# Exponentials per head straight from PSUM with bias and sum, a scaled magnitude of the weight words, and lo parts of two weight matrices on VectorE in the first tile

## The chip, the core and the metric

The kernel runs on one core of one Trainium2 chip. A core has a matrix engine (TensorE, PE, which loads a stationary operand, then streams a moving one and writes to PSUM), a vector engine (VectorE, DVE), an engine for pointwise functions (ScalarE, ACT), a general engine (GpSimd, POOL) and a queue engine (SyncE, SP) that here issues all the DMAs. Each engine takes its own instructions in the order of the program and waits by semaphores for the others. The metric is device time in microseconds, the median of several runs. The profile is of one execution.

## The reference

Attention over pooled keys and values, and a feed-forward layer on its output. Cut to what is computed:

```python
# q, k, v: (8 batches, 8 heads, 576, 64) float32; pool = 8, Sp = 72
k_p = k.reshape(B, H, Sp, pool, D).mean(axis=3)
v_p = v.reshape(B, H, Sp, pool, D).mean(axis=3)
scores = scale * np.matmul(q, k_p.transpose(0, 1, 3, 2))
scores = scores - np.max(scores, axis=-1, keepdims=True)
attn = np.exp(scores)
attn = attn / (np.sum(attn, axis=-1, keepdims=True) + 1e-09)
out = np.matmul(attn, v_p)                     # then (B*S, H*D) = (4608, 512)
...
a = x @ w_a                                    # 512 -> 1536
b = x @ w_b
return (a * b @ w_out).astype(np.float32)      # 1536 -> 512
```

The weights reach the kernel as 64-bit floats, seen as pairs of 32-bit words, and the kernel makes 32-bit floats of them.

## The kernel before

**Two parts for every operand.** Each matrix product is made of three matmuls: every operand is split into a hi part, a copy to the matmul's type (ACT), and a lo part, what is left of it, a subtraction (`low_part`, L170, on DVE or POOL as its caller says). The products are hi by hi, hi by lo and lo by hi, summed in PSUM.

**The feed-forward part.** The 4608 rows are nine tiles of 512. For each tile, twelve steps x run over the 1536 middle columns in blocks of 128 (`ffn_in`, L539, and `ffn_out`, L560). A step has 12 matmuls into `psa`, 12 into `psb` and, for the step before, 12 into the four `acc` banks; ACT copies `psa` to `h` (L555), DVE multiplies `h` by `psb` (L528), ACT and DVE make the parts `hh` and `hl` (L531, L171). `split_weight` makes the parts of the weight blocks, `jh` on ACT (L236) and `jl` on POOL (L238, recorded as L171), anew for each tile.

**The weights' conversion.** Only in the first tile, `convert_weights` turns the words of 36 blocks (twelve each of `a`, `b`, `o`) into floats: ACT takes the magnitude of the high word (L212) and scales the low word (L213), DVE limits and scales the magnitude (L214), masks and shifts it (L215), puts the sign back (L219) and adds the low word (L224). The load of the next block's words (L222) follows L219, as the words have one buffer per matrix.

**The attention part.** The rows of a batch are five chunks of 128 rows, one of them with 64; there are 40 chunks, and `chunk(i)` carries one from its queries to the transposed probabilities. Chunks 0 to 4 come before the first tile's feed-forward, the others are spread between the matmuls of the tile before the one that needs them. The scores of a chunk are made from `kdiag`, the pooled keys of two heads side by side in hi and lo parts. Chunks below SUMMED = 9 make them in two halves of four heads, 6 matmuls of 144 columns each, and take maximum and difference from PSUM (L374, L375 in `less_max`). Chunks from 9 on use per pair of heads one matmul of 288 columns (the query's hi part by both parts of the keys side by side) and one of 144, add the two halves of columns on DVE (L410), and then take maximum and difference for all heads from SBUF. Then one exponential for all eight heads (L424, ACT), the sum (L426), 1e-9 and the reciprocal (L427, L428, DVE), the product (L430, POOL mostly), the parts of the probabilities `pr` and `rem` (L439, L441 on ACT, lo parts on POOL), and the transposes on PE (L475, copied out by ACT at L476). Scores, transposes and values of later chunks share two PSUM buffers of the tag `att`.

**What sets the order.** The order is written out by hand. `Chains` holds generators; `chains.step()` is called six times in each step x, every six matmuls, and resumes the chains that are due. `yield n` puts the rest of a chain n steps later, `yield PE` waits for a turn to put matmuls into the stream (one chain a step in the feed-forward part). What a chain issues between two yields stands together in the program, and each engine meets it in that order.

Of the kernel before, what the change touches and what calls it, by code (L numbers as in the profile page):

```python
# [9 lines left out]
F32 = mybir.dt.float32  # L10
F32R = mybir.dt.float32r
I32 = mybir.dt.int32
U32 = mybir.dt.uint32
AF = mybir.ActivationFunctionType
ALU = mybir.AluOpType
# [5 lines left out]
P = 128  # L21
# [7 lines left out]
TINY = 2.0**-15  # L29
# [25 lines left out]

SUMMED = 9
# [57 lines left out]
def attn_moe_kernel(ctx: ExitStack, tc: tile.TileContext, q, k, v, vr, wa, wb, wo, out):  # L114
# [55 lines left out]
    def low_part(eng, lo, src, hi):  # L170
        eng.tensor_tensor(out=lo, in0=src, in1=hi.bitcast(F32), op=ALU.subtract)  # L171
# [23 lines left out]
    def convert_weights(name, j, first):  # L195
# [4 lines left out]

# [5 lines left out]
        for f in range(NF):  # L206
# [5 lines left out]
            nc.scalar.activation(mag, hi.bitcast(F32), AF.Abs)  # L212
            nc.scalar.activation(low, lo.bitcast(U32), AF.Copy, scale=2.0**-29)  # L213
            nc.vector.tensor_scalar(out=w, in0=mag, scalar1=TINY, scalar2=2.0**-16, op0=ALU.max, op1=ALU.mult)  # L214
            nc.vector.tensor_scalar(  # L215
                out=wi, in0=wi, scalar1=0x0FFFFFFF, scalar2=3, op0=ALU.bitwise_and, op1=ALU.logical_shift_left
# [14 lines left out]
    def split_weight(name, x):  # L231
# [6 lines left out]
        low_part(nc.gpsimd, lo, raw[name][:, f, :], hi)  # L238
# [107 lines left out]
    def chunk(i):  # L346
# [25 lines left out]
        def less_max(hs, src):  # L372
            nh = hs.stop - hs.start
            nc.vector.tensor_reduce(out=m[:n, hs], in_=src, axis=AX.X, op=ALU.max)  # L374
            nc.vector.tensor_tensor(  # L375
                out=s[:n, hs], in0=src, in1=m[:n, hs].unsqueeze(2).broadcast_to([n, nh, SP]), op=ALU.subtract
            )

        if i < SUMMED:
            for g0 in range(0, NK, 2):  # L380
                yield from wait(("keys", b, g0))
                yield PE
                if first:
                    pt = ps.tile([P, 512], F32, tag="acc", name=f"psc_{i}_{g0}", bufs=4)
                else:
                    pt = ps.tile([P, 512], F32, tag="att", name=f"psc_{i}_{g0}", bufs=2)
                for j in range(2):
                    g = g0 + j
                    for x, (qq, w) in enumerate(((qh, 0), (qh, 1), (ql, 0))):
                        nc.tensor.matmul(  # L390
                            pt[:n, j * hk:(j + 1) * hk],
                            qq[:, g, :n],
                            kd[:, g, w].rearrange("p e s -> p (e s)"),
                            start=(x == 0),
                            stop=(x == 2),
                        )
                less_max(slice(2 * g0, 2 * g0 + 4), pt[:n, :2 * hk].rearrange("p (h s) -> p h s", h=4))
        else:
            for g in range(NK):
                yield from wait(("keys", b, g - g % 2))  # L400
                if g % 2 == 0:
                    yield PE
                pt = ps.tile([P, 512], F32, tag="att", name=f"psc_{i}_{g}", bufs=2)
                nc.tensor.matmul(  # L404
                    pt[:n, :2 * hk], qh[:, g, :n], kd[:, g].rearrange("p w e s -> p (w e s)"), start=True, stop=False
                )
                nc.tensor.matmul(
                    pt[:n, :hk], ql[:, g, :n], kd[:, g, 0].rearrange("p e s -> p (e s)"), start=False, stop=True
                )
                nc.vector.tensor_reduce(  # L410
                    out=s[:n, 2 * g:2 * g + 2, :].rearrange("p h s -> p (h s)"),
                    in_=pt[:n, :2 * hk].rearrange("p (w c) -> p c w", w=2),
                    axis=AX.X,
                    op=ALU.add,
                )
                if g % 2 and g < NK - 1:
                    yield 1
            yield 1
            less_max(slice(0, H), s[:n])
# [264 lines left out]
```

## Time and profile before

| | |
|---|---|
| median of 3 runs | 1110.5 us (1110.24 to 1191.36) |
| the profiled execution | 1109.42 us, its span 1107.6 us |
| mean granted clock of PE | 0.972 |
| busy, share of the span | PE 94%, weight loads 78%, DVE 54%, ACT 47%, POOL 51% |
| the chain that ended last | PE 82%, DVE 13%, ACT 2% of the span |
| read from memory, written | 49.28 MB, 9.44 MB |

A line of the profile has the program's line, the engine, the operation, the tile written and the tiles read, and the shapes. Busy time is the sum of the durations; matmuls overlap in the records, so two of them follow each other faster than one lasts, and PE's pace is read from start to start. Shares over the whole span mix stages with different limits, so that the stage has to be named with each number.

### The profile page before, as it was taken

Reading aid. Unit: us, or ns where it says so; the run is one execution under the profiler, and the core shown is the slowest. Engines: PE = TensorE matmul, PEld = TensorE weight load, DVE = VectorE, ACT = ScalarE, POOL = GpSimd, SP = SyncE. Lnnn points to the kernel's source line nnn. Section 1 sums busy time; section 2 is a strip of 40 time slices with the busy share of each in tenths; the row PEclk is TensorE's granted clock in tenths of the full one; section 3 lists DMA queues with packets and bytes.
Section 4 is the critical chain, followed back from the end, with each engine's and each line's share of the span. In section 5 each row is a group of like instructions: output and inputs, shape, how many; then the busy total and the mean of one; then the engine's idle time right before and its main releaser. Section 6 shows DMA issues by size and latency. Waiting matters only on the chain.

```text
span 1107.6 us, 13659 instructions
## 1 busy us (share of the span) xinstructions
PE 1036.8 (94%) x4964; PEld 861.5 (78%) x4964; DVE 601.3 (54%) x953; ACT 523.2 (47%) x1051; POOL 565.4 (51%) x465
## 2 busy tenths in 40 slices
PE   4378887899999999999999999999999999999998
PEld 4256765688887888888888888888888888888887
DVE  8889899963348333753367335653458343332111
ACT  3654555544445445544455445444445444443332
POOL 6234353455555555555555455554556455554442
PEclk9778888999999999999999999999999999999999
DMA  6444343220023000400021002200211020001001
GB/s 221 124 142 124 121 129 120 74 89 1 1 70 111 1 1 22 148 3 1 1 94 59 1 1 91 81 1 1 69 55 48 1 67 1 1 1 38 1 1 38
DMA packets 29875, 59.59 MB, mean 54 GB/s; under 512 B 7121, under 2 KB 7121, under 8 KB 29809
## 3 DMA queue, kind: packets, MB, share of 16 engines
q1 hardware_dynamic: 29808, 58.73, 16.7%
q8 instruction: 39, 0.64, 0.2%
q14 instruction: 28, 0.22, 0.1%
HBM read 49.28 MB, written 9.44 MB: 53 GB/s over the span
## 4 chain that ended last, share of the span: by engine, by line
PE 82%; DVE 13%; ACT 2%; DMA 1%; issue 1%; POOL 0%; SPq 0%; DVEq 0%; ACTq 0%
PE acc L571 9%; PE psa L550 8%; PE psb L550 8%; PE acc L573 8%; PE acc L572 8%; PE psa L552 8%; PE psa L551 8%; PE psb L551 8%; PE psb L552 8%; PE ptr L475 2%; PE psc L404 2%; DVE wb_raw L224 1%; DVE wa_raw L224 1%; DVE wo_raw L224 1%; DVE wb_raw L219 1%
## 5 line engine op out<-in xcount | busy, mean ns | idle before, releaser
L171 POOL TENSOR_TENSOR jlb<-wb_raw,jhb 128x512 fp32r<-128x512 f32 x108 | 142.8, 1322 | 244.6 <-ACT jhb L236 244.6
L528 DVE TENSOR_TENSOR h<-psb,h 128x512 f32<-128x512 f32 x108 | 74.5, 690 | 344.1 <-PE psb L552 334.3
L171 POOL TENSOR_TENSOR jla<-wa_raw,jha 128x512 fp32r<-128x512 f32 x108 | 143.1, 1325 | 196.4 <-ACT jha L236 170.1
L555 ACT COPY h<-psa 128x512 f32<-128x512 f32 x108 | 63.3, 587 | 241.9 <-PE psa L552 234.3
L550 PE MATMUL psb<-xh,jhb 128*128 128x512 f32 x432 | 172.9, 400 | 4.6 <-DVE h L528 4.6
L571 PE MATMUL acc<-jho,hh 128*128 128x512 f32 x432 | 175.7, 407 | 0.0
L550 PE MATMUL psa<-xh,jha 128*128 128x512 f32 x432 | 172.7, 400 | 0.0
L573 PE MATMUL acc<-jho,hl 128*128 128x512 f32 x432 | 170.2, 394 | 0.6 <-DVE hl L171 0.6
L572 PE MATMUL acc<-jlo,hh 128*128 128x512 f32 x432 | 170.0, 393 | 0.0
L552 PE MATMUL psb<-xh,jlb 128*128 128x512 f32 x432 | 170.0, 393 | 0.0
L551 PE MATMUL psb<-xl,jhb 128*128 128x512 f32 x432 | 169.9, 393 | 0.0
L552 PE MATMUL psa<-xh,jla 128*128 128x512 f32 x432 | 169.6, 392 | 0.0
L551 PE MATMUL psa<-xl,jha 128*128 128x512 f32 x432 | 169.3, 392 | 0.0
L171 POOL TENSOR_TENSOR jlo<-wo_raw,jho 128x512 fp32r<-128x512 f32 x108 | 154.3, 1428 | 5.6 <-ACT jho L236 5.6
L531 ACT CAST hh<-h 128x512 fp32r<-128x512 f32 x108 | 67.1, 621 | 84.7 <-DVE h L528 84.6
L171 DVE TENSOR_TENSOR hl<-h,hh 128x512 fp32r<-128x512 f32 x108 | 93.9, 869 | 20.7 <-ACT hh L531 20.5
L550 PEld LDWEIGHTS psb<-xh,jhb 128*128 128x128 f32 x432 | 82.2, 190 | 20.9 <-issue 4.3
L573 PEld LDWEIGHTS acc<-jho,hl 128*128 128x128 f32 x432 | 81.9, 190 | 18.9 <-DVE hl L171 1.0
L552 PEld LDWEIGHTS psb<-xh,jlb 128*128 128x128 f32 x432 | 82.2, 190 | 17.6
L552 PEld LDWEIGHTS psa<-xh,jla 128*128 128x128 f32 x432 | 81.7, 189 | 17.6
L551 PEld LDWEIGHTS psb<-xl,jhb 128*128 128x128 f32 x432 | 82.2, 190 | 15.2
L551 PEld LDWEIGHTS psa<-xl,jha 128*128 128x128 f32 x432 | 82.0, 190 | 15.2 <-DVE xl L171 0.2
(92 smaller groups left out, 1714.4 us busy)
## 6 DMA issues: line engine op xcount, KB each, us to landing
out<-y SPq DMA_DIRECT2D x36, 256.0 KB, 2.2
kraw<-in_k SPq DMA_DIRECT2D x28, 288.0 KB, 3.6
vraw<-in_v SPq DMA_DIRECT2D x28, 256.0 KB, 3.0
qraw<-in_q SPq DMA_DIRECT2D x28, 256.0 KB, 3.7
words<-in_wa SPq DMA_DIRECT2D x12, 512.0 KB, 3.5
words<-in_wb SPq DMA_DIRECT2D x12, 512.0 KB, 3.6
words<-in_wo SPq DMA_DIRECT2D x12, 512.0 KB, 3.5
vraw<-in_vr SPq DMA_DIRECT2D x14, 192.0 KB, 2.5
```

Source lines behind the costliest of these rows:

```text
L171: eng.tensor_tensor(out=lo, in0=src, in1=hi.bitcast(F32), op=ALU.subtract)
L224: nc.vector.tensor_tensor(out=wi, in0=wi, in1=low, op=ALU.add)
L404: nc.tensor.matmul(pt[:n, :2 * hk], qh[:, g, :n], kd[:, g].rearrange("p w e s -> p (w e s)"), start=True, stop=False)
L528: nc.vector.tensor_tensor(out=h, in0=pt, in1=h, op=ALU.mult)
L531: nc.scalar.copy(hh, h)
L550: nc.tensor.matmul(pt, wh[:, c], xh[:, kk], start=(kk == 0), stop=False)
L551: nc.tensor.matmul(pt, wh[:, c], xl[:, kk], start=False, stop=False)
L552: nc.tensor.matmul(pt, wl[:, c], xh[:, kk], start=False, stop=(kk == NK - 1))
L555: nc.scalar.copy(h, pt)
L571: nc.tensor.matmul(acc[c], hh[:, cs], wh, start=(f == 0), stop=False)
L572: nc.tensor.matmul(acc[c], hh[:, cs], wl, start=False, stop=False)
L573: nc.tensor.matmul(acc[c], hl[:, cs], wh, start=False, stop=(f == NF - 1))
```

## The change

Four things change.

1. In `convert_weights` the magnitude is scaled by 2^-112 in ACT's instruction, and the DVE instruction that limited it from below and scaled it (L214) is gone; the mask and the shift read ACT's result directly.
2. In `split_weight` the lo parts of `a` and `b` are made on VectorE for the twelve blocks of the first tile. Those of `o`, and all of the later tiles, stay on GpSimd.
3. All chunks make their scores as chunks 0 to 8 did, in two halves of four heads; SUMMED and the other way are gone.
4. In each half DVE takes the maximum and multiplies it by -SCALE; ACT then makes one exponential per head, from PSUM, with that as its bias and with the sum over the head's 72 columns as a second output. The difference, the one exponential over all heads and DVE's sum are gone, and with them two places where the chain gave way for a step.

```diff
-TINY = 2.0**-15
+SHRINK = 2.0**-112
...
-SUMMED = 9
...
-            nc.scalar.activation(mag, hi.bitcast(F32), AF.Abs)
+            nc.scalar.activation(mag, hi.bitcast(F32), AF.Abs, scale=SHRINK)
             nc.scalar.activation(low, lo.bitcast(U32), AF.Copy, scale=2.0**-29)
-            nc.vector.tensor_scalar(out=w, in0=mag, scalar1=TINY, scalar2=2.0**-16, op0=ALU.max, op1=ALU.mult)
             nc.vector.tensor_scalar(
-                out=wi, in0=wi, scalar1=0x0FFFFFFF, scalar2=3, op0=ALU.bitwise_and, op1=ALU.logical_shift_left
+                out=wi, in0=mag.bitcast(I32), scalar1=0x0FFFFFFF, scalar2=3, op0=ALU.bitwise_and, op1=ALU.logical_shift_left
             )
...
-        low_part(nc.gpsimd, lo, raw[name][:, f, :], hi)
+        low_part(nc.vector if x < NF and name != "o" else nc.gpsimd, lo, raw[name][:, f, :], hi)
...
-        def less_max(hs, src):
-            nh = hs.stop - hs.start
-            nc.vector.tensor_reduce(out=m[:n, hs], in_=src, axis=AX.X, op=ALU.max)
-            nc.vector.tensor_tensor(
-                out=s[:n, hs], in0=src, in1=m[:n, hs].unsqueeze(2).broadcast_to([n, nh, SP]), op=ALU.subtract
-            )
-
-        if i < SUMMED:
-            for g0 in range(0, NK, 2):
...
-                less_max(slice(2 * g0, 2 * g0 + 4), pt[:n, :2 * hk].rearrange("p (h s) -> p h s", h=4))
-        else:
-            for g in range(NK):
...
-            yield 1
-            less_max(slice(0, H), s[:n])
+        for g0 in range(0, NK, 2):
+            yield from wait(("keys", b, g0))
+            yield PE
+            if first:
+                pt = ps.tile([P, 512], F32, tag="acc", name=f"psc_{i}_{g0}", bufs=4)
+            else:
+                pt = ps.tile([P, 512], F32, tag="att", name=f"psc_{i}_{g0}", bufs=2)
+            for j in range(2):
+                g = g0 + j
+                for x, (qq, w) in enumerate(((qh, 0), (qh, 1), (ql, 0))):
+                    nc.tensor.matmul(
+                        pt[:n, j * hk:(j + 1) * hk],
+                        qq[:, g, :n],
+                        kd[:, g, w].rearrange("p e s -> p (e s)"),
+                        start=(x == 0),
+                        stop=(x == 2),
+                    )
+            hs = slice(2 * g0, 2 * g0 + 4)
+            scores = pt[:n, :2 * hk].rearrange("p (h s) -> p h s", h=4)
+            nc.vector.tensor_reduce(out=m[:n, hs], in_=scores, axis=AX.X, op=ALU.max)
+            nc.vector.tensor_scalar_mul(m[:n, hs], m[:n, hs], -SCALE)
+            for j in range(4):
+                h = 2 * g0 + j
+                nc.scalar.activation(
+                    s[:n, h], scores[:, j], AF.Exp, bias=m[:n, h:h + 1], scale=SCALE, accum_out=z[:n, h:h + 1]
+                )
         mark("scores", i)
 
 
         yield 1
-        nc.scalar.activation(s[:n], s[:n], AF.Exp, scale=SCALE)
-        yield 1
-        nc.vector.tensor_reduce(out=z[:n], in_=s[:n], axis=AX.X, op=ALU.add)
         nc.vector.tensor_scalar_add(z[:n], z[:n], 1e-9)
         nc.vector.reciprocal(z[:n], z[:n])
         yield 1
```

More of the change, by code (lines that the diff above doesn't have):

```diff
@@ L370, in chunk @@
         hk = 2 * SP
-        def less_max(hs, src):
-            nh = hs.stop - hs.start
-            nc.vector.tensor_reduce(out=m[:n, hs], in_=src, axis=AX.X, op=ALU.max)
-            nc.vector.tensor_tensor(
-                out=s[:n, hs], in0=src, in1=m[:n, hs].unsqueeze(2).broadcast_to([n, nh, SP]), op=ALU.subtract
-            )
-        if i < SUMMED:
-            for g0 in range(0, NK, 2):
[L381 to L384, printed above, removed]
-                else:
[L386 to L396, printed above, removed]
-                less_max(slice(2 * g0, 2 * g0 + 4), pt[:n, :2 * hk].rearrange("p (h s) -> p h s", h=4))
-        else:
-            for g in range(NK):
[L400 to L405, printed above, removed]
-                )
[L407 to L416, printed above, removed]
-                    yield 1
-            yield 1
-            less_max(slice(0, H), s[:n])
@@ L420, in chunk @@
         mark("scores", i)
         yield 1
-        nc.scalar.activation(s[:n], s[:n], AF.Exp, scale=SCALE)
-        yield 1
-        nc.vector.tensor_reduce(out=z[:n], in_=s[:n], axis=AX.X, op=ALU.add)
         nc.vector.tensor_scalar_add(z[:n], z[:n], 1e-9)
```

## The prediction

> **What bounds the kernel now.** I read the page's slices first, then the table by stage, then who waited in the slow stage, and only then single groups.
>
> ```profile
> span 1107.6 us, 13659 instructions
> PE   4378887899999999999999999999999999999998
> DVE  8889899963348333753367335653458343332111
> PEclk9778888999999999999999999999999999999999
> ```
>
> The reader is to see two stages. In the first eight slices VectorE (DVE) is at 8 or 9 tenths, and TensorE (PE) is neither full nor at full clock. From then on PE is at 9 to the end and DVE at 3 to 7. The table by stage gives it in microseconds (columns: busy time of PE, weight loads, DVE, ACT, POOL, each with its count; then the granted clock and the DMA share):
>
> ```profile
> core 0: us, PE busy (x) PEld busy (x) DVE busy (x) ACT busy (x) POOL busy (x), PEclk, DMA share, GB/s
> 36.00:60.00 24.00, 8.99 (x50) 8.31 (x49) 19.55 (x33) 12.04 (x24) 4.32 (x4) 0.64 0.57 178
> 60.00:216.00 156.00, 123.57 (x550) 98.64 (x548) 142.12 (x208) 85.59 (x170) 67.08 (x49) 0.86 0.38 119
> 216.00:1107.60 891.60, 887.66 (x4295) 739.70 (x4294) 409.04 (x659) 408.90 (x820) 472.77 (x382) 1.00 0.11 34
> ```
>
> From 36 to 216 us, the first tile with its weight conversion, DVE is busy 161.7 of 180 us (19.55 and 142.12). What DVE no longer does there comes off the end nearly one for one. After 216 us PE is busy 887.66 of 891.60 us at full clock: what DVE, ACT or POOL save there is worth nothing, and each microsecond added to PE is paid in full. The change must be read against both stages.
>
> **The change part by part: VectorE in the first tile.** Each row below comes from a line's own view (count: shortest/median/longest ns), and the row under it is that line's busy DVE time in the window 36 to 216 us.
>
> ```profile
> L214 DVE TENSOR_SCALAR wa_raw<-wmag_a x12: 367/420/1516, 34.9 to 194.6; 128x512 f32<-128x512 f32 x12
> 36.00:216.00 180.00, 19.53 (x35) 0.83 0.41 127
> ...
> L215 DVE TENSOR_SCALAR wa_raw<-wa_raw x12: 426/427/2510, 35.3 to 195.0; 128x512 int32<-128x512 int32 x12
> 36.00:216.00 180.00, 20.83 (x35) 0.83 0.41 127
> ...
> L219 DVE SCALAR_TENSOR_TENSOR wa_raw<-words,wa_raw x12: 641/694/1810, 36.3 to 195.5; 128x512 int32<-128x512 int32 x12
> 36.00:216.00 180.00, 31.87 (x36) 0.83 0.41 127
> ...
> L224 DVE CUSTOM_DVE_ANT_0 wa_raw<-wa_raw,wlow_a x12: 691/693/3084, 37.8 to 197.4; 128x1024 uint16<-128x1024 uint16 x12
> 36.00:216.00 180.00, 39.60 (x36) 0.83 0.41 127
> ```
>
> (a) The words' magnitude. L214 goes from DVE: 19.53 us in the window. ACT's L212 takes the scale as one more immediate of an instruction that is there already, so I add nothing to it; at a tenth of its length more, ACT, far from full here, would cover it. The load of the next words (L222, on SP's queue) is issued behind L219 and so a little earlier; the pace of the conversion is held by `begun`, not by the load.
>
> (b) The lo parts of `a` and `b` for x below 12 go from POOL to DVE, 24 instructions. The nearest DVE row is `hl`, the same operation, shape and types:
>
> ```profile
> L171 POOL TENSOR_TENSOR jla<-wa_raw,jha x13: 1264/1296/1717, 41.1 to 214.5; 128x512 fp32r<-128x512 f32 x13
> L171 POOL TENSOR_TENSOR jlo<-wo_raw,jho x11: 1269/1705/1743, 68.2 to 211.3; 128x512 fp32r<-128x512 f32 x11
> L171 DVE TENSOR_TENSOR hl<-h,hh x11: 676/684/1786, 76.5 to 214.3; 128x512 fp32r<-128x512 f32 x11
> L171 DVE TENSOR_TENSOR hl<-h,hh 128x512 fp32r<-128x512 f32 x11 | 9.7, 879 | 0.0
> ```
>
> Between its median and its mean, 0.78 us, 24 cost 18.7 us (bounds 16.4 at 0.684 and 21.1 at 0.879). Alone, (a) and (b) nearly cancel.
>
> (c) What comes with (b): DVE instructions here have two lengths. L224 takes 0.693 us or up to 3.08, L215 0.427 or up to 2.51. Over their medians, L215 has 20.83 - 35 x 0.427 = 5.9 us, L219 31.87 - 36 x 0.694 = 6.9 and L224 39.60 - 36 x 0.693 = 14.7: 27.5 us of waiting inside DVE instructions, in lumps of about the 1.3 us that a POOL subtraction takes. I read it as DVE and POOL keeping each other out. POOL has 53 instructions in these 180 us (4 and 49); 24 go, so I take 24/53 of 27.5 = 12.4 us off. Bounds: 0, if the other POOL work meets DVE instead, and 27.5.
>
> By the Trainium skill (SBUF — State Buffer, "Who interferes with whom") a VectorE instruction with two SBUF inputs, or in a 2-port mode, and a GpSimd instruction that reads SBUF exclude each other for a whole instruction, and whichever starts first wins. The two lengths agree with it. It also says that the moved subtractions, having two SBUF inputs, stay exposed to `jlo`, which is why I did not price them at the bare median.
>
> (d) Softmax on DVE, chunks 0 to 8:
>
> ```profile
> L426 DVE TENSOR_REDUCE z<-s x9: 736/741/754, 16.1 to 190.1; 128x8 f32<-128x576 f32 x7, 64x8 f32<-64x576 f32 x2
> L375 DVE TENSOR_TENSOR s<-psc,m x18: 450/458/459, 11.4 to 186.9; 128x288 f32<-128x288 f32 x14, 64x288 f32<-64x288 f32 x4
> L374 DVE TENSOR_REDUCE m<-psc x18: 441/448/458, 10.9 to 186.4; 128x4 f32<-128x288 f32 x14, 64x4 f32<-64x288 f32 x4
> L427 DVE TENSOR_SCALAR z<-z x9: 162/172/1032, 16.9 to 190.9; 128x8 f32<-128x8 f32 x7, 64x8 f32<-64x8 f32 x2
> 0.00:36.00 36.00, 2.64 (x4) 1.00 0.55 178
> 36.00:216.00 180.00, 1.53 (x5) 0.83 0.41 127
> ```
>
> Gone: 9 x 0.741 + 18 x 0.458 = 14.9 us. New: 18 small multiplications by -SCALE, whose nearest row is L427 (its busy time stands under it: 4.17 us for nine, 0.46 each): 8.3 us. Net -6.6 us; bounds -11.8 (all at 0.172) and +3.7 (all at 1.032). L374 stays. The skill's rule in that section speaks against the change here: the subtraction that goes reads PSUM and by the rule never meets POOL (450 to 459 ns agrees), while the multiplication that comes works from SBUF and can be held (162 to 1032 ns agrees); if every one were held, the end would be 10.3 us later than by my mean.
>
> DVE in the first 216 us: -19.5 + 18.7 - 12.4 - 6.6 = -19.8 us, taken as **-20**.
>
> **ACT.** One exponential per chunk becomes eight, of 72 elements, with a pointer bias and a sum. The trace has no such instruction; the nearest are the small copy and the exponential itself:
>
> ```profile
> L441 ACT CAST rem<-s 128x64 fp32r<-128x64 f32 x64 | 12.4, 241 | 0.0
> L424 ACT ACTIVATE s<-s 128x576 f32<-128x576 f32 x32 | 22.0, 688 | 45.0 <-DVE s L375 44.8
> ```
>
> The two give 0.87 ns an element, so at least 0.25 us each; writing out the sum at most another instruction of that size, 0.50. A gain is excluded, as one 688 ns instruction is all that goes. Between the ends I take 0.4, nearer the upper one, since bias and sum both come on top: eight take 3.2 us, 2.5 more per chunk. For the 31 later chunks that is 78 us on an engine busy 409 of 892; for the first nine 23 us. Hidden as busy time, but not as latency: ACT now waits in program order for PE's scores, DVE's maximum and the new multiplication, twice per chunk, with the weights' copies, `h` and `hh` queued behind; DVE's L427 waits for the eight in turn, with PSUM evictions behind it. If ACT had no room the first tile would get the 23 us back.
>
> The Trainium skill (ScalarE: Activation LUTs, "What ACT_TABLE_LOAD costs") gives 280 ns + 0.833 per element with a pointer bias and about 93 ns of overlap, an estimated 0.25 us at 72 elements; it has no price for the sum. By it eight cost 2.0 us and the sum of the forecast is the same.
>
> **TensorE after 216 us.** With SUMMED gone, chunks 9 to 39 form scores as the first nine did: per half six matmuls of 144 columns in place of two of 288 and two of 144. First matmul of a half and the first one behind it, new form and then old form, both at full clock in the feed-forward stream:
>
> ```profile
> 183.33 0.34 PE L390 MATMUL psc<-kdiag,qh 128*128 128x144 f32 x2
> 183.96 0.43 PE L550 MATMUL psb<-xh,jhb 128*128 128x512 f32 x1
> ...
> 217.94 0.29 PE L404 MATMUL psc<-kdiag,qh 128*128 128x288 f32 x1
> 218.39 0.44 PE L550 MATMUL psb<-xh,jhb 128*128 128x512 f32 x1
> ...
> L404 PE MATMUL psc<-kdiag,qh x124: 293/295/403, 215.6 to 969.9; 128*128 128x288 f32 x100, 128*64 128x288 f32 x24
> ```
>
> 0.63 against 0.45 us: +0.18 per half. The 100 full matmuls of L404 are 50 halves: **+9.0 us**; the 24 on 64 rows I put at nothing (at the same 0.18 they would add 2.2). No cover: PE is the bound.
>
> **The latency behind it.** The new code drops two steps between scores and transposes. In an old chunk:
>
> ```profile
> 410.76 0.29 PE L404 MATMUL psc<-kdiag,qh 128*128 128x288 f32 x1
> 417.69 0.20 DVE L428 RECIPROCAL z<-z 128x8 f32<-128x8 f32 x1
> 421.92 0.32 POOL L171 TENSOR_TENSOR rem<-s,rem 128x64 fp32r<-128x64 f32 x1
> 424.00 0.46 PE L475 MATMUL ptr<-ident,pr 128*128 128x128 f32 x4
> 425.77 0.47 PE L475 MATMUL ptr<-ident,pr 128*128 128x128 f32 x4
> ```
>
> The reciprocal ends at +7.1, the lo parts at +11.5, the second transposes start at +15.0. Two steps of about 1.4 us fewer (36 matmuls make six steps) and 0.36 us more PE work put those at +12.6, so the reciprocal must end by 12.6 - 4.4 = +8.2. New: scores 0.6, maximum and multiplication 0.9, eight exponentials 3.2, three other ACT copies between them at some 0.6, z 0.4: about +7. It fits with 1 us to spare. The PSUM buffers (two, `att`) are held through the exponentials; where a 64-row chunk follows closely on another they may be missed. I add **+2 us** for such places (bounds 0 and 8, some 2 us at four places).
>
> **Sum.** The profiled execution took 1109.4 us (span 1107.6), 1.1 below the median of 1110.5. 1109.4 - 20 + 9 + 2 = 1100.4, so 1100.
>
> **The rivals.**
> - *More of the waiting inside DVE goes, and PE's clock with it.* For: PEclk is 0.86 there, and the lumps sit in the pairs that move. Against: 29 POOL instructions stay. With all 27.5 us gone instead of 12.4: 1085. Chance 0.17. By the skill's exclusion rule the lumps cannot go while `jlo` stays, which is why this is not higher.
> - *ACT becomes the late one in the first tile* (its waits for the maxima hold up `jha`, which DVE now waits for in order, where POOL waited before). For: 45 us of idle before L424 already. Against: ACT is busy only 85.6 of 156. If three quarters of the gain are lost: 1109.4 - 5 + 11 = 1115. Chance 0.17.
> - *Slower: PE waits for the transposes in every later chunk.* The place is ptr L475; it starts when the eight exponentials push the reciprocal past +8.2, at about 0.55 us each, and every further 0.1 us costs 0.8 us x 31 = 25 us. At 0.75 us each: 1150; the limit of slower is crossed near 0.7. Against: my upper row gives 0.50. Chance 0.08.
> - *The exchange does nothing*: gains and PE's 11 us just cancel, 1109. It lies within the forecast's own range.
>
> **How the numbers follow.** Forecast 1100, chance 0.58, own range 1092 to 1109. With the rivals at 1085 and 1115 inside, the range is 1084 to 1118; it leaves out the slower case and some of the tails, about 0.2. Two per cent, about what a measurement of this kernel can tell from no change, is 22 us: faster means below 1088, slower above 1133. Faster 0.19 (the first rival and the edge of the forecast), slower 0.09, same 0.72.
>
> **What would show it.** L214 gone; 24 lo parts on DVE near 0.7 to 0.8 us; means of L219 and L224 lower by a third to a half; first-tile stage ending near 196 us instead of 216; PE from there to the end 11 us longer, with halves of 0.63 us; eight exponentials per chunk of 0.25 to 0.5 us; no ptr wait on PE after the first tile. I am wrong if the stage ends after 210 us (ACT), or if ptr L475 waits in most chunks, or if the 144-column halves cost PE no more than before.

## The result, and the profile after

The changed kernel takes 1118.9 us (median of 4 runs, 1116.7 to 1121.0) against 1111.0 us for the kernel before in the same comparison: a ratio of 1.0073, 95% interval 1.0048 to 1.0099. It is within 2%, on the slow side, and 0.9 us above the predicted range. One of the four runs before took 1191.4 us in a slow state of the chip; its median counts this run, the ratio does not, and the same holds for one run of e9 below (1465.5 us, at a granted clock of 0.67). The profiled execution of the changed kernel took 1116.7 us, with a span of 1115.0 us.

The first view of the changed kernel's page is the busy table and the slices, as quoted of before:

```profile
span 1115.0 us, 14406 instructions
...
PE   4387888999998999999999999999999999999998
...
DVE  7688888632455225632456335643356333332111
...
PEclk9989889999999999999999999999999999999999
```

The reader is to see that VectorE's run of 8s and 9s is shorter and lower than before, and that PE's slices behind it look the same but for one 8, the slice from 334 to 362 us. At this grain no more of the loss is visible. I cut both traces at the same three events instead: the first feed-forward matmul of step 0, the first one of step 12 (the end of the first tile), and the last matmul. Columns as in the prediction's table by stage, first of before, then of after:

```profile
59.70:223.90 164.20, 131.63 (x588) 105.38 (x588) 149.88 (x220) 89.12 (x177) 70.29 (x51) 0.86 0.37 113
223.90:1103.40 879.50, 879.50 (x4258) 733.21 (x4257) 400.63 (x647) 405.17 (x814) 469.56 (x379) 1.00 0.11 33
```

```profile
59.90:209.20 149.30, 127.72 (x591) 101.89 (x591) 123.88 (x207) 100.99 (x268) 37.16 (x29) 0.92 0.40 125
209.20:1110.70 901.50, 892.41 (x4378) 745.80 (x4377) 377.12 (x553) 457.64 (x1263) 477.44 (x380) 1.00 0.10 33
```

The first tile became 14.9 us shorter (164.2 to 149.3), the rest 22.0 us longer (879.5 to 901.5). Their sum, with 0.2 us at the start, is the 7.4 us by which the span grew. So there are two questions. In the first tile DVE's busy time fell by 26.0 us (149.88 to 123.88), yet the stage by only 14.9: the idle time of DVE, length less busy, rose from 14.3 to 25.4 us. And in the rest PE has 12.9 us more busy time (892.41 against 879.50) and 9.1 us in which it does nothing, where before it had none.

**First tile: who waits.** The list of waits from 36 us to the end of that stage (microseconds in all, times, longest), first of before, then of after:

```profile
DVE wa_raw L214 <- ACT wmag_a L212: 2.8, 3, 1.3
DVE wo_raw L214 <- ACT wmag_o L212: 2.4, 3, 1.0
DVE wb_raw L214 <- ACT wmag_b L212: 2.0, 2, 1.3
...
ACT s L424 <- DVE s L375: 11.9, 5, 4.3
```

```profile
ACT s L392 <- DVE m L389: 20.6, 11, 3.9
...
DVE z L399 <- ACT s L392: 7.8, 6, 1.5
DVE wa_raw L212 <- ACT wmag_a L210: 5.6, 3, 3.4
DVE wo_raw L212 <- ACT wmag_o L210: 5.3, 3, 2.5
DVE wb_raw L212 <- ACT wmag_b L210: 4.9, 3, 1.9
```

DVE waits 15.8 us for ACT's magnitudes where it waited 7.2, and 7.8 us for the sums, a wait it did not have. ACT in turn stands 20.6 us before exponentials, waiting for DVE's maxima. The two engines wait for each other in turn. The program puts the words' magnitudes behind exponentials on ACT, so one that waits for its maximum holds them up; e8 tests how much of the loss this is.

**The rest: halves and transposes.** The halves cost what the prediction read off chunks 0 to 8 (first matmul of a half, and the first one behind it, in the timeline of after):

```profile
257.50 0.35 PE L379 MATMUL psc<-kdiag,qh 128*128 128x144 f32 x2
...
258.13 0.44 PE L522 MATMUL psa<-xh,jha 128*128 128x512 f32 x1
```

0.63 us. The list of waits from 220 us on has this PE row, and that of before has none for the same stretch:

```profile
PE ptr L447 <- ACT p L448: 7.7, 5, 3.5
```

The timeline of after around one of these waits (start, length, instruction, and in brackets the idle time before it), by engine:

```profile
335.57 1.49 POOL L402 TENSOR_TENSOR s<-s,z 64x576 f32<-64x576 f32 x1 [4.40 <-DVE z L400]
337.02 1.29 POOL L170 TENSOR_TENSOR jla<-wa_raw,jha 128x512 fp32r<-128x512 f32 x1
338.40 1.36 POOL L170 TENSOR_TENSOR pr<-s,pr 64x512 fp32r<-64x512 f32 x1
339.71 0.33 POOL L170 TENSOR_TENSOR rem<-s,rem 64x64 fp32r<-64x64 f32 x1
339.99 1.28 POOL L170 TENSOR_TENSOR jlb<-wb_raw,jhb 128x512 fp32r<-128x512 f32 x1
341.24 1.25 POOL L170 TENSOR_TENSOR jlo<-wo_raw,jho 128x512 fp32r<-128x512 f32 x1
...
335.97 6.81 DVE L328 SCALAR_TENSOR_TENSOR vdiag<-vp,vdiag 64x256 fp32r<-64x256 f32 x2
342.70 0.68 DVE L170 TENSOR_TENSOR vrem<-vwide,vrem 32x512 fp32r<-32x512 f32 x1
343.41 0.69 DVE L500 TENSOR_TENSOR h<-psb,h 128x512 f32<-128x512 f32 x1
...
344.13 0.62 ACT L503 CAST hh<-h 128x512 fp32r<-128x512 f32 x1 [4.18 <-DVE h L500]
344.66 0.64 ACT L448 CAST p<-ptr 128x256 fp32r<-128x256 f32 x2
...
345.17 0.36 PE L447 MATMUL ptr<-ident,rem 64*96 64x64 f32 x2 [3.52 <-ACT p L448]
```

Read from the bottom: PE stands 3.52 us at the third group of transposes, which needs a buffer that ACT's copies of the first two groups (L448) must free. ACT had been idle for 4.18 us, but these copies stand behind `hh`, which waits for `h` from DVE. And DVE is in two small instructions on the values' diagonals (`vdiag`), 6.81 us for the two. Meanwhile, from 335.57 to 342.49 us, POOL works through six instructions with gaps of at most 0.1 us: the product of a 64-row chunk, its two lo parts and the weights' three. The line's own view (count, then shortest/median/longest ns, 300 to 1100 us) gives a `vdiag` a median of 1.68 us after, and below it, from the trace of before, 0.42:

```profile
L328 DVE SCALAR_TENSOR_TENSOR vdiag<-vp,vdiag x10: 915/1684/4149, 336.0 to 853.6; 64x256 fp32r<-64x256 f32 x10
```

```profile
L331 DVE SCALAR_TENSOR_TENSOR vdiag<-vp,vdiag x10: 404/422/1461, 345.4 to 846.8; 64x256 fp32r<-64x256 f32 x10
```

In the trace the diagonals are made once for each batch, at six places from 208 us on. At three of them a 64-row chunk's share of POOL falls on them, and the two instructions take 4.3 to 6.8 us; at the other three it is the weights' subtractions beside a 128-row chunk, and they take 2.4 us. That the two dropped steps moved this work there was at this point a reading of one trace. The experiments had to test it, and to divide the 22.0 us.

The wait of 3.52 us has a tail. Before it PE's feed-forward matmuls start every 0.23 us, behind it (346.05, 346.48, 346.90 us and on) every 0.43 us, and the granted clock there is half. A second such stretch comes after the wait of 1.55 us that ends at 858.72 us (windows, same columns):

```profile
345.17:348.30 3.13, 3.13 (x9) 2.38 (x10) 0.31 (x1) 0.91 (x3) 1.28 (x1) 0.50 0.00 0
860.30:863.60 3.30, 3.30 (x14) 2.67 (x13) 0.61 (x2) 1.30 (x8) 0.87 (x1) 0.51 0.00 0
```

Outside these two stretches no microsecond from 210 to 1100 us has a clock under 0.96, and in the traces of before, of e4 and of e5 none has one under 0.97. At half the clock these 6.4 us do the work of 3.2, so a part of the loss stands in PE's busy time and not in its waits. A wait of 1.54 us at 601 us has no such stretch behind it; what sets one off is not shown.

### The profile page after: what moved, and what is told of

It reads as the page before. It is cut to its first block, busy times and chain, and to the rows that moved or that the text cites. A ratio compares the mean times of both kernels' runs of the same rounds, so it can differ in the third digit from the quotient of the medians.

```text
span 1115.0 us, 14406 instructions
## 1 busy us (share of the span) xinstructions
PE 1045.9 (94%) x5088; PEld 870.9 (78%) x5088; DVE 543.8 (49%) x839; ACT 594.8 (53%) x1651; POOL 538.6 (48%) x441
## 3 DMA queue, kind: packets, MB, share of 16 engines
q1 hardware_dynamic: 29808, 58.73, 16.5%
## 4 chain that ended last, share of the span: by engine, by line
PE 78%; DVE 13%; ACT 6%; issue 2%; DMA 1%; SPq 0%; DVEq 0%; ACTq 0%
PE psb L522 8%; PE psa L522 8%; PE psa L524 8%; PE psa L523 8%; PE acc L543 8%; PE acc L544 8%; PE acc L545 8%; PE psb L524 8%; PE psb L523 7%; PE psc L379 3%; ACT s L392 3%; DVE vdiag L328 2%; PE ptr L447 2%; DVE vrem L170 1%; DVE h L500 1%
## 5 line engine op out<-in xcount | busy, mean ns | idle before, releaser
L170 POOL TENSOR_TENSOR jlb<-wb_raw,jhb 128x512 fp32r<-128x512 f32 x96 | 125.1, 1303 | 201.2 <-ACT jhb L233 201.2
L522 PE MATMUL psb<-xh,jhb 128*128 128x512 f32 x432 | 177.8, 412 | 1.3 <-DVE h L500 1.3
L543 PE MATMUL acc<-jho,hh 128*128 128x512 f32 x432 | 171.5, 397 | 0.0
L392 ACT ACTIVATE s<-psc,m 128x72 f32<-128x72 f32 (+1 forms) x320 | 97.9, 318 | 133.1 <-DVE m L389 131.7
L170 POOL TENSOR_TENSOR jla<-wa_raw,jha 128x512 fp32r<-128x512 f32 x96 | 138.4, 1442 | 44.1 <-ACT jha L233 43.7
L402 POOL TENSOR_TENSOR s<-s,z 128x576 f32<-128x576 f32 (+1 forms) x38 | 46.1, 1213 | 223.7 <-PE psb L524 141.0
L170 DVE TENSOR_TENSOR hl<-h,hh 128x512 fp32r<-128x512 f32 x108 | 125.8, 1165 | 38.2 <-ACT hh L503 38.0
L543 PEld LDWEIGHTS acc<-jho,hh 128*128 128x128 f32 x432 | 81.9, 190 | 16.2
```

Source lines behind the costliest of these rows:

```text
L392: nc.scalar.activation(s[:n, h], scores[:, j], AF.Exp, bias=m[:n, h:h + 1], scale=SCALE, accum_out=z[:n, h:h + 1])
L402: (nc.vector if first and i % 2 else nc.gpsimd).tensor_tensor(out=s[:n], in0=s[:n], in1=z[:n].unsqueeze(2).broadcast_to([n, H, SP]), op=AL ...
L522: nc.tensor.matmul(pt, wh[:, c], xh[:, kk], start=(kk == 0), stop=False)
L543: nc.tensor.matmul(acc[c], hh[:, cs], wh, start=(f == 0), stop=False)
```

## The experiments

All twelve experiments, first as a table. The first tile and the rest are the lengths between the events named above, from each profiled execution. The kernel before is at 1110.5 to 1110.6 us in each comparison. Parts 1 to 4 are those of the section on the change.

| kernel | first tile | rest | median us | ratio, 95% interval |
|---|---|---|---|---|
| before | 164.2 | 879.5 | 1110.5 | 1 |
| after | 149.3 | 901.5 | 1118.9 | 1.0073 (1.0048 to 1.0099) |
| e1 parts 1 and 2 | 145.1 | 879.5 | 1088.8 | 0.9800 (0.9785 to 0.9815) |
| e2 after, later chunks as before | 148.9 | 879.6 | 1094.3 | 0.9850 (0.9835 to 0.9864) |
| e3 after, chunks 0 to 8 as before | 144.8 | 903.0 | 1112.6 | 1.0018 (1.0008 to 1.0027) |
| e4 part 3 alone | 164.7 | 889.0 | 1120.2 | 1.0082 (1.0065 to 1.0099) |
| e5 after, two steps put back | 148.8 | 892.2 | 1108.2 | 0.9981 (0.9972 to 0.9991) |
| e6 after, later products on DVE | not cut | 900.3 | 1113.2 | 1.0039 (1.0021 to 1.0056) |
| e7 part 1 alone | 149.5 | 879.6 | 1096.6 | 0.9881 (0.9865 to 0.9898) |
| e8 e2, exponentials a step later | 145.1 | 879.6 | 1089.5 | 0.9816 (0.9801 to 0.9832) |
| e9 part 2 alone | 156.2 | 879.6 | 1101.7 | 0.9921 (0.9901 to 0.9941) |
| e10 after, corrections of e5 and e8 | 143.0 | 892.3 | 1102.3 | 0.9927 (0.9910 to 0.9944) |
| e11 e1, all three lo parts on DVE | 141.6 | 879.5 | 1085.2 | 0.9779 (0.9761 to 0.9797) |
| e12 e11, new softmax in chunks 0 to 8 | 143.0 | 879.6 | 1088.3 | 0.9799 (0.9783 to 0.9816) |

### e1: parts 1 and 2 alone

The kernel before with the first two parts; scores and softmax stay as they were.

```diff
-            nc.scalar.activation(mag, hi.bitcast(F32), AF.Abs)
+            nc.scalar.activation(mag, hi.bitcast(F32), AF.Abs, scale=SHRINK)
...
-            nc.vector.tensor_scalar(out=w, in0=mag, scalar1=TINY, scalar2=2.0**-16, op0=ALU.max, op1=ALU.mult)
...
-        low_part(nc.gpsimd, lo, raw[name][:, f, :], hi)
+        low_part(nc.vector if x < NF and name != "o" else nc.gpsimd, lo, raw[name][:, f, :], hi)
```

> The kernel before with parts 1 and 2 alone (scaled magnitude, lo parts of a and b on VectorE in the first tile), softmax as before. Theory A (in the changed kernel VectorE's work of the first tile fell by 27 us, but 12 of them came back as idle time because ScalarE, held by the new exponentials, is late): without the exponentials VectorE falls by about 22 us and its idle time stays near 18, so twelve steps end near 204 us of the span instead of 223.9, and the time is near 1091 us. Rival B (the idle time is the next limit, the loads of the words and the pace of the steps, and comes whoever relieves VectorE): twelve steps end near 210 us and the time is near 1097 us.

Measured: 1088.8 us, with the twelfth step ending at 203.9 us: theory A. The two stages of its trace, same columns:

```profile
58.80:203.90 145.10, 126.53 (x588) 101.82 (x587) 131.58 (x212) 88.86 (x177) 38.87 (x29) 0.93 0.42 128
203.90:1083.40 879.50, 879.50 (x4258) 733.25 (x4257) 399.20 (x647) 405.14 (x814) 470.07 (x379) 1.00 0.10 33
```

The rest is that of before, and the first tile is 19.1 us shorter. All of the change's gain sits in parts 1 and 2. Against this kernel, the new scores and softmax take another 7.7 us of busy time off DVE in the first tile (131.58 to 123.88), but the stage gets 4.2 us longer, because the idle time of DVE goes from 13.5 to 25.4 us.

### e2 and e3: the new softmax in one stage only

In e2 chunks 9 to 39, in e3 chunks 0 to 8 go back to the scores and softmax of before; the rest is the changed kernel.

```diff
-        for g0 in range(0, NK, 2):
-            yield from wait(("keys", b, g0))
...
+        if i < SUMMED:
+            for g0 in range(0, NK, 2):
+                yield from wait(("keys", b, g0))
...
+        else:
+            for g in range(NK):
+                yield from wait(("keys", b, g - g % 2))
```

(e3 has `i >= SUMMED` in the first condition. After the `else` both have the code of before, shortened here.)

> The changed kernel, but chunks 9 to 39 form scores and softmax as before. Theory: the first tile is as in the changed kernel (13 to 15 us gained) and the 22 us lost after it are gone, so about 1097 us. Rival: part of the later loss is a shift that the first tile hands on; then it stays above 1105 us.

> The changed kernel, but chunks 0 to 8 have the softmax as before, so the first tile is that of parts 1 and 2 alone, and chunks 9 to 39 have the new one. Theory A: first tile as in the run with parts 1 and 2 alone (near 204 us at twelve steps), then 22 us lost: about 1113 us. Rival B: first tile near 210 us, 1119 us.

Measured: 1094.3 us, 3 us less than its theory said, and 1112.6 us, as theory A said. The rest of e2 is 879.6 us, that of before, and that of e3 is 903.0, near that of after (901.5); the first tiles are 148.9 and 144.8 us. The new softmax costs in both places: some 4 us in the first tile, where it was to gain 6.6, and, with the halves, some 22 us later.

### e4: part 3 alone

All chunks form their scores in two halves, with the softmax and the steps of before.

```diff
-SUMMED = 9
+SUMMED = 40
```

> The kernel before with the scores of all chunks in halves of six matmuls, maximum and difference from PSUM as chunks 0 to 8 do, one exponential, sum on VectorE; one step fewer from scores to transposes than before, two more instructions of VectorE per chunk, no other part of the change. Theory: the halves cost 0.18 us each, 9 to 10 us in all, and no long waits of transposes come: 1120 to 1121 us, with the six-transpose groups near their 17.7 us in all. Rival (the long waits come with the dropped step and not with the exponentials on ScalarE): 1126 to 1131 us, with single waits over 1 us at the transposes of the 64-row chunks.

Measured: 1120.2 us, 9.7 more than before, and in the trace

```profile
224.90:1113.90 889.00, 888.27 (x4378) 742.74 (x4377) 373.64 (x583) 403.41 (x812) 471.82 (x380) 1.00 0.10 33
```

9.5 us more than before (889.00 against 879.50), with PE busy all but 0.7 us of it. These are the halves, and one of the two dropped steps goes with them, as the expectation says; by itself it brings no long waits. Of the 22.0 us, 12.5 are left for what the halves are not: 8.4 us more in which PE does nothing (9.1 against 0.7) and 4.1 us more in which it is busy (892.41 against 888.27), of which the two stretches at half clock are some 3.2.

### e5: the two dropped steps put back

```diff
         mark("scores", i)
-        yield 1
+        yield 1 if i < 9 else 3
         nc.vector.tensor_scalar_add(z[:n], z[:n], 1e-9)
```

> The changed kernel with the two dropped steps put back for chunks 9 to 39, ahead of the addition of 1e-9, so that product, parts and transposes are issued where they were before. The changed kernel lost 10 us at the third group of transposes of six chunks (single waits of 1.2 to 4.8 us). Theory S (the waits come from the dropped steps, which bring two chunks' work and a batch's values together): the waits go and the time falls by some 10 us, to 1108 to 1110 us. Rival P (they come from GpSimd's instructions piling up behind the product that waits for the sums, and VectorE being shut out while the pile runs off): part of it stays, as the product still waits for the eight sums, but with more time; 1112 to 1119 us.

Measured: 1108.2 us, 10.7 below the changed kernel. The second stage, the view of `vdiag` (300 to 1100 us), and the list of PE's waits from 225 us on:

```profile
209.80:1102.00 892.20, 888.67 (x4378) 742.66 (x4377) 347.99 (x553) 457.61 (x1262) 464.93 (x380) 1.00 0.10 33
```

```profile
L328 DVE SCALAR_TENSOR_TENSOR vdiag<-vp,vdiag x10: 407/420/1409, 332.8 to 842.1; 64x256 fp32r<-64x256 f32 x10
```

```profile
PE ptr L447 <- ACT s L392: 2.6, 3, 1.0
PE ptr L447 <- ACT p L448: 1.0, 1, 1.0
```

With the steps back, the median of `vdiag` returns to 0.42 us and the long waits are gone, and the stretches at half clock with them: 9.3 of the 12.5 us (901.5 to 892.2). DVE's busy time in the rest falls by 29.1 us for the same 553 instructions (377.12 to 347.99), which is time that they had been held. The other 3.2 us (892.2 against e4's 889.0) remain, and the waits that remain, 3.6 us, now mostly end with ACT's exponentials. The steps are thus most of this loss, and what remains with them put back, the exponentials' waits among it, is the smaller part.

### e6: the later products on VectorE

A rival for the same waits: POOL's instructions pile up because the product (1.49 us) is first in POOL's queue. Here DVE makes it for chunks 9 to 39.

```diff
-        (nc.vector if first and i % 2 else nc.gpsimd).tensor_tensor(
+        (nc.vector if i >= 9 or first and i % 2 else nc.gpsimd).tensor_tensor(
```

> The changed kernel with the product by the reciprocal on VectorE for chunks 9 to 39, so GpSimd no longer waits for the sums and nothing piles up behind it; the steps stay as in the changed kernel. Theory P (the pile shuts VectorE out): the two subtractions of the values' diagonal, 6.8 and 4.3 us before the long waits, go back to under 2 us for both, the waits go, 1108 to 1110 us. Rival S (the dropped steps): the waits at the same places stay within a few us in all, 1117 to 1121 us.

Measured: a rest of 900.3 us in the profiled execution (901.5 for the changed kernel), and `vdiag` still long:

```profile
L328 DVE SCALAR_TENSOR_TENSOR vdiag<-vp,vdiag x10: 413/1513/4171, 338.2 to 852.5; 64x256 fp32r<-64x256 f32 x10
```

In this execution, taking the product away from POOL does not open the run; the lo parts and the weights' three subtractions are enough to keep DVE out, and PE's clock is at half twice, as after the change. But the runs took 1113.1, 1113.1, 1113.2, 1116.8 and 1117.1 us, and the profiled one is the longest of them. The median is 5.7 us below the changed kernel's, between the two forecasts. The rival is refuted for the traced execution only; what the three shorter runs did otherwise has no trace, and a share of the product in the loss is not excluded.

### e7 and e9: parts 1 and 2 each by itself

e7 is the kernel before with the first two edits of e1 (the scaled magnitude, no L214), e9 the kernel before with the third one (the lo parts of `a` and `b` on DVE).

> The kernel before with part 1 alone (scaled magnitude, one VectorE instruction fewer per block). By the prediction's terms part 1 is worth 19.5 us and the lo parts on VectorE cost 6 net of the contention they take away: about 1091 us, near the 1088.8 us of both parts together. Rival: the lo parts on VectorE carry a share, because what they take off the contention (20 us of the 47 us above the shortest durations) is more than what they cost; then part 1 alone is 1095 to 1101 us.

> The kernel before with part 2 alone (lo parts of a and b on VectorE in the first tile). The prediction's terms b and c for it: 24 more instructions on VectorE at 0.78 us, 12.4 us of waiting inside VectorE's instructions gone, so 6 us later, 1116 to 1117 us. Rival (VectorE's busy time comes out even, 17 us added and as much contention taken away, and shorter queues on GpSimd bring the other parts earlier): 1103 to 1109 us.

Measured: 1096.6 us (13.9 below before), in its rival's range, and 1101.7 us (8.8 below), below both ranges. Together that is 22.7, and e1, which has both, gains 21.7: the parts add up. The first stage of e7, and then of e9, same columns:

```profile
59.50:209.00 149.50, 126.22 (x588) 100.75 (x587) 132.81 (x189) 89.33 (x177) 72.10 (x51) 0.93 0.40 123
```

```profile
59.50:215.70 156.20, 131.16 (x588) 104.08 (x587) 143.30 (x241) 89.33 (x177) 38.16 (x29) 0.88 0.38 119
```

In e7 DVE loses 17.1 us of busy time (149.88 to 132.81) and gains 2.4 us of idle time (14.3 to 16.7); the stage is 14.7 us shorter. e9 is the surprise. The groups of its lo parts in that stage (busy us, mean ns, idle before):

```profile
L171 DVE TENSOR_TENSOR jla<-wa_raw,jha 128x512 fp32r<-128x512 f32 x11 | 7.6, 694 | 0.0
...
L171 DVE TENSOR_TENSOR jlb<-wb_raw,jhb 128x512 fp32r<-128x512 f32 x11 | 7.5, 683 | 0.0
```

15.1 us of work were added to the engine that bounds the stage, and its busy time fell by 6.6 us (149.88 to 143.30). So 21.7 us went from other DVE instructions; 0.7 of it is one that falls outside this cut, and 16.5 are on the conversion's L215, L219 and L224, which have the same number of instructions in both (81.3 and 64.8 us). The stage is 8.0 us shorter: 6.6 of busy time and 1.4 of idle time, so work that came earlier from a shorter queue on POOL can be no more than the small part. That these instructions no longer wait for the subtractions on POOL shows in the last operation on the words of `b`, first before, then in e9:

```profile
L224 DVE CUSTOM_DVE_ANT_0 wb_raw<-wb_raw,wlow_b x12: 691/1476/1841, 44.0 to 203.4; 128x1024 uint16<-128x1024 uint16 x12
```

```profile
L224 DVE CUSTOM_DVE_ANT_0 wb_raw<-wb_raw,wlow_b x12: 691/693/1422, 43.7 to 195.2; 128x1024 uint16<-128x1024 uint16 x12
```

At the median, an instruction that had been held for 0.78 us is held no more.

### e8: the exponentials a step later in the first tile

If the first tile's loss is ACT standing at exponentials whose maxima are not there, a step between maximum and exponentials (chunks 5 to 8) should give it back. The edit is made to e2, so that the later chunks do not blur it (`first` stands for chunks 0 to 4).

```diff
             nc.vector.tensor_scalar_mul(m[:n, hs], m[:n, hs], -SCALE)
+            if not first:
+                yield 1
             for j in range(4):
```

> As the run with the new softmax in chunks 0 to 8 only (1094.3 us), but chunks 5 to 8 issue the exponentials of a half one step after its maximum, as the kernel before did with its one exponential. Theory (in the first tile ScalarE stands at the exponentials until VectorE has done the maximum, and the words' magnitudes queue behind): VectorE's idle time falls from 28 us towards the 18 us of the run without exponentials, and the time falls from 1094 to 1089 to 1091 us. Rival (the exponentials' own 2.4 us per chunk on ScalarE are what delays): no change, 1093 to 1096 us.

Measured: 1089.5 us, 4.9 below e2, with the first stage down from 148.9 to 145.1 us (e2, then e8):

```profile
59.40:208.30 148.90, 123.95 (x588) 98.16 (x588) 125.92 (x207) 97.91 (x252) 37.88 (x29) 0.95 0.41 125
61.20:206.30 145.10, 126.02 (x588) 100.93 (x588) 124.25 (x206) 97.65 (x252) 38.07 (x29) 0.93 0.42 128
```

The time came as expected, the reason only in part: DVE's idle time went from 23.0 us (148.90 less 125.92 busy, in e2) to 20.9, not down to e1's 13.5. ACT's waits for the maxima, from 36 to 210 us, fell from 17.7 to 14.0 us. So the place of the exponentials costs the 3.8 us, which the time shows, but with DVE busy 7.3 us less than in e1 (124.25 against 131.58) the stage is just as long as there. What holds it at 145 us is then not DVE's busy time alone. The chain of work that ended last points at the expectation's rival, the exponentials' own time: they are 7.9% of this stage's chain in e8, some 11 us, where the old exponentials are 2 us of it in e1. No run varied that time, so what holds the stage stays open.

### e10: both corrections on the changed kernel

```diff
             nc.vector.tensor_scalar_mul(m[:n, hs], m[:n, hs], -SCALE)
+            if early <= i < 9:
+                yield 1
             for j in range(4):
...
-        yield 1
+        yield 1 if i < 9 else 3
```

> The changed kernel with both placements mended: two steps put back for chunks 9 to 39, and in chunks 5 to 8 the exponentials one step after the maximum. Theory: the two corrections add up (10.7 us and 4 to 5 us), 1103 to 1105 us; what stays against the 1088.8 us of parts 1 and 2 alone is the 9.6 us of six matmuls in place of four per half, and 4 to 6 us of waits. Rival: they take from the same waits, 1107 to 1109 us.

Measured: 1102.3 us, slightly below its range, with 143.0 and 892.3 us for the two stages. Against the changed kernel that is 6.3 and 9.2 us, and the rest is that of e5. What separates it from before in the rest is 12.8 us: 9.5 for the halves (e4) and 3.3 for what e5 left. The halves stay whatever the order.

### e11: all three lo parts on VectorE, the softmax of before

The reasons above point to a kernel that beats both: keep parts 1 and 2, drop 3 and 4, and move the remaining one of the first tile's weight subtractions too.

```diff
-        low_part(nc.vector if x < NF and name != "o" else nc.gpsimd, lo, raw[name][:, f, :], hi)
+        low_part(nc.vector if x < NF else nc.gpsimd, lo, raw[name][:, f, :], hi)
```

> Parts 1 and 2 with the lo parts of o on VectorE too in the first tile, softmax as before. Theory (each POOL subtraction in the first tile costs VectorE about what it costs to do it there): VectorE's busy time within 3 us of that with two matrices, 1085 to 1090 us, against 1088.8 us. Rival (what is left of the contention comes from the parts of the probabilities and the products, not from o): 8 us more on VectorE, 1094 to 1097 us.

Measured: 1085.2 us, as its theory said, ratio 0.9779 (0.9761 to 0.9797): the shortest of all, and the only one whose whole interval is beyond 2%. The first stage:

```profile
57.40:199.00 141.60, 127.09 (x588) 102.35 (x588) 130.10 (x225) 90.76 (x179) 20.33 (x17) 0.91 0.43 131
```

Twelve more subtractions, and DVE is busy 130.10 us where it was 131.58 in e1. The pattern of e9 holds for `o` as well.

### e12: e11 with the new softmax in chunks 0 to 8

e11 with part 4 for the first nine chunks (e8's extra step among it), the later ones as before.

```diff
         if i < SUMMED:
...
-                less_max(slice(2 * g0, 2 * g0 + 4), pt[:n, :2 * hk].rearrange("p (h s) -> p h s", h=4))
+                hs = slice(2 * g0, 2 * g0 + 4)
...
+                if not first:
+                    yield 1
+                for j in range(4):
```

> The lo parts of all three matrices on VectorE in the first tile, scaled magnitude, new softmax for chunks 0 to 8 with the exponentials of chunks 5 to 8 one step after the maximum, chunks 9 to 39 as before. Theory (in the first tile the new softmax, well placed, takes some 5 us off VectorE and gives as much back in waits for ScalarE, so it is worth nothing beside the other two parts): 1083 to 1088 us, no different from the 1085.2 us without it. Rival (with VectorE relieved further, the softmax's relief shows): 1078 to 1082 us.

Measured: 1088.3 us, 3.1 above e11 and just past its theory's range, though the runs overlap (1087.2 to 1088.7, and 1084.5 to 1089.1 in e11). The first stage has DVE busy 123.66 us, 6.4 less than in e11, and lasts 143.0 us, 1.4 longer. With this softmax, that saving on DVE bought nothing.

## Why the prediction was right or wrong

The change was forecast as 10 us faster and came out 8 us slower: 1118.9 us for 1100, beyond the range. That it stayed within 2%, as was most likely, is no merit of the mechanism: a gain and a loss cancel, but not in the sizes forecast. The sum was 1109.4 - 20 + 9 + 2 = 1100.4, and the profiled execution took 1116.7. Of the 16.3 us between them the latency term has 10.5, the VectorE term 5.1 and the halves 0.5. The terms, one by one:

**The -20 on VectorE: right for the busy time, wrong for the stage.** DVE's busy time fell by more, 26.0 us, and the stage by 14.9. The step that failed is "what DVE no longer does there comes off the end nearly one for one". 11.1 us came back as idle time of DVE; in the lists above it waits 16.4 us more for ACT than before (magnitudes and sums). The prediction named the place ("hidden as busy time, but not as latency", with DVE's L427 waiting for the exponentials and PSUM evictions behind it) and gave it no term; the rival that ACT becomes the late one had it, at 0.17 and for three quarters of the gain. e8 shows that the placing of the exponentials costs 3.8 us of the stage (148.9 to 145.1); the cause of the rest is open. The sign set for it, a stage that ends after 210 us, was set against an end at 216 us before; by the events used here the end moved from 223.9 to 209.2 us and the sign did not fire. Within the term:
- (a) L214 was put at -19.5; e7 measured -17.1 in DVE's busy time (16.5 of L214's busy time lie in this stage) and -13.9 in the time.
- (b) and (c) were put at +18.7 - 12.4, a loss of 6.3; e9 measured a gain of 8.8. The lo parts cost 0.69 us for 0.78 taken. On the three lines that (c) counted, 16.5 us went, not 12.4, and some 4.5 more on lines that it did not count, `hl` for one. Counting POOL's instructions (24 of 53) undersized it: it matters which ones meet DVE, and in this order those for `a` and `b` met it more than their number says. The rule of the Trainium skill that was weighed there (SBUF — State Buffer, "Who interferes with whom") agrees with `b`'s L224, which fell from 1476 to 693 ns at the median. The conclusion drawn from it, that the lumps could not go while `jlo` stays, was too strong: e9 left `jlo` on POOL, and 16.5 of the 26.9 us that these lines had above their medians in this stage went.
- (d) -6.6 was right for the busy time (-7.7 between e1 and after), and the new multiplication is cheaper than the 0.46 us taken: on 128 rows 0.17 us in the first tile and 0.21 in the whole kernel, by these groups (the first from the window 36 to 210 us, the second from the whole span). But it was not right for the time: e1 to after, the stage got 4.2 us longer.

```profile
L389 DVE TENSOR_SCALAR m<-m 128x4 f32<-128x4 f32 x8 | 1.4, 170 | 0.3
...
L389 DVE TENSOR_SCALAR m<-m 128x4 f32<-128x4 f32 x64 | 13.4, 209 | 2.2
```

**ACT's 0.4 us per exponential: inside its bounds, a quarter too high.** An exponential of the new form is two records, the function and the reading of the sum, and they overlap the next one (groups, then the timeline of one chunk):

```profile
L392 ACT ACTIVATE s<-psc,m 128x72 f32<-128x72 f32 x256 | 78.5, 321 | 110.6 <-DVE m L389 109.4 <-PE psa L524 1.2
L392 ACT ACTIVATION_READ_ACCUMULATOR s<-psc,m 128x1 f32 x256 | 52.5, 205 | 0.0
```

```profile
331.28 0.32 ACT L392 ACTIVATE s<-psc,m 64x72 f32<-64x72 f32 x1 [2.21 <-DVE m L389]
331.50 0.19 ACT L392 ACTIVATION_READ_ACCUMULATOR s<-psc,m 64x1 f32 x1
331.59 0.30 ACT L392 ACTIVATE s<-psc,m 64x72 f32<-64x72 f32 x1
```

From one start to the next it takes 0.31 us here, inside the bounds of 0.25 and 0.50. The rival in which PE waits in every later chunk for the exponentials (1150 us) did not come.

**The +9 on TensorE: right.** e4 measured 9.5 in the stage and 9.7 in the time, and leaving out the 64-row halves was no error that can be seen.

**The +2 for the latency: wrong, 12.5 in its place, and beyond its bound of 8.** The deadline of +8.2 us was worked out for one chunk by itself, and for most chunks it fits: PE's list has five waits for 31 chunks. The step that failed here is to work out one chunk's deadline alone and leave out what the two dropped steps move the chunk's work onto. Once in each batch a run of POOL, a chunk's instructions and the weights', now stands where DVE makes the diagonals of the values, and DVE is kept out; `h`, `hh`, the copies and the third transposes follow. e5 takes this away with two steps: 9.3 us. The loss was also larger than the waits, as PE's clock was at half for 6.4 us, which the prediction did not reckon with. Its test ("if ptr L475 waits in most chunks") did not fire, as five waits in the list were enough; its milder sign, no ptr wait after the first tile, did fail.

In sum: 1109.4 - 14.9 + 9.5 + 12.5, with 0.2 at the start, is 1116.7, the profiled execution's time. Of the 12.5, e5 shows 9.3 to be the steps; of the other 3.2 it is only seen that most of the waits left in e5 end with the exponentials.

## What to carry to other kernels

Before pricing a move between two engines that lock each other out, look at which instructions meet in time, not at how many there are: taking a POOL subtraction to the fuller engine made that engine emptier. Work on an in-order engine must be placed where its inputs are ready, or whatever is queued behind it pays. And when steps are dropped from a hand-written order, look at what the shifted work lands on, on every engine and also at places that come only once a batch; the time of the chunk by itself does not show it. And when the engine that bounds a stage stands idle, look at its clock behind the wait too.

## What the runs showed of the hardware

- A VectorE instruction of 0.42 us can be held through several GpSimd instructions in a row, not one: the two on `vdiag` took 6.81 us, the second 4.15 us of it, while POOL ran six instructions from 335.57 to 342.49 us. The Trainium skill (SBUF — State Buffer, "Who interferes with whom") tells of a lock for a whole instruction, won by whichever comes first; here, as the trace has it, the next POOL instruction took the turn more than once.
- 15.1 us of subtractions moved from GpSimd to VectorE took some 21 us off the other VectorE instructions (e9).
- After waits of PE of 3.52 and 1.55 us in the changed kernel its granted clock was 0.50 and 0.51 for 3.1 and 3.3 us, at once in the first case and 1.6 us later in the second; after another of 1.54 us it was not.
- An exponential with a sum as second output leaves a second record on ScalarE, 205 ns on 128 partitions, that overlaps the next one in part.
